# One row-block load of two weight matrices in a fused convolution and max-out kernel, and the order of its opening

## The chip, the core and the metric

The kernel runs on one core of a Trainium2 chip. The core has a matrix engine (TensorE, "PE" in the profile), a vector engine (VectorE, "DVE"), a scalar engine (ScalarE, "ACT"), GpSimd ("POOL") and SyncE ("SP"), which here only issues transfers. Sixteen DMA engines move data between memory (HBM) and the on-chip buffer SBUF; TensorE writes its results to PSUM, from which ScalarE and VectorE copy them. Each engine works through its own queue of instructions in order and waits on semaphores of the others. The metric is device time in microseconds for one launch, lower is better.

## What is computed

```python
def _attn_ref(x, weight_gen):            # x (8, 4160, 192), weight_gen (8, 4160, 8, 7)
    w = weight_gen - np.max(weight_gen, axis=-1, keepdims=True)
    w = np.exp(w)
    w = w / (np.sum(w, axis=-1, keepdims=True) + 1e-09)
    x_pad = np.concatenate([np.zeros((B, 6, D)), x], axis=1)
    idx = np.arange(S)[:, None] + np.arange(7)[None, :]
    x_unf = x_pad[:, idx, :].reshape(B, S, 7, 8, 24)
    return np.einsum('bshk,bskhg->bshg', w, x_unf).reshape(B, S, D)

def _moe_ref(x, w1, w2, w_out):          # w1, w2 (192, 1024), w_out (1024, 192)
    h1 = x @ w1
    h2 = x @ w2
    g = np.maximum(h1, h2)
    return g @ w_out
```

The second function is applied to the first one's result: a convolution over the last seven positions with weights that a softmax gives for each position and head, and then two products whose larger value, element by element, goes through a third. All arrays are float32; 33280 positions of 192 features in all.

## The kernel before

**Tiling.** The 33280 positions are laid on 128 partitions with 260 columns each. Columns are taken in 17 batches, of 16 columns but for the last two (12 and 8); batches 0 and 1 are cut into pieces of four columns, the later ones of eight. A batch goes through: an exponential of its weights (ScalarE, `exp_sum`, L153), a sum (VectorE, `red`, L168), a logarithm (ScalarE, `ln`, L172), a subtraction (VectorE, `shift`, L177) and a second exponential (ScalarE, `weights`, L191), which gives the softmax; then a product with seven shifted views of x (VectorE, `mul`, L211). For batches 0 and 1 the sum over the seven taps and the transposition are done by matmuls with an identity (`sum_transpose`, L281), copied out of PSUM by ScalarE (`sums_out`, L293).

**The max-out.** max(h1, h2) is computed as h1 + relu(h2 - h1). So w2 - w1 is formed on VectorE (`diff`, L593), the hidden product uses that difference (`hid_tile`, L336), ScalarE applies the relu (`relu`, L346), and the result is multiplied by w_out (`out_hidden`, L375). The h1 part needs only x @ (w1 @ w_out): w1 is cast (L611), transposed on TensorE (`w1_products`, L628), copied (L633), multiplied by w_out (`w10_product`, L647) and copied again (L654, L656), and enters at L387.

**The weights in blocks.** w1 and w2 have 192 rows of 1024 columns. Their first 128 rows go to one buffer each (`ws0E`, `ws1E`), in two halves of 512 columns (`load_w`, L562). The last 64 rows go to a second buffer of 128 partitions by 512 (`ws0T`, `ws1T`): columns 0 to 511 on partitions 0 to 63, columns 512 to 1023 on partitions 64 to 127, each by a transfer of its own (`load_last`, L570). `diff(i)` makes block i of the difference: 0 and 1 from the two halves of the first rows, 2 from the last rows. `wd` has six blocks of 512 columns; blocks 3, 4 and 5 are blocks 0, 1 and 2 with their partition halves exchanged, made by a matmul with a rotated identity into PSUM (`turn`, L601) and a copy out of it (`turn_out`, L607). Hidden features 0 to 511 read blocks 0, 2, 3 and 5; features 512 to 1023 read 1, 2, 4 and 5. With pieces of four columns a piece has four hidden tiles, of two feature chunks each: tiles 0 and 1 of a piece cover features 0 to 511, tiles 2 and 3 the others.

**What sets the order.** The kernel's engines follow the order in which the program names the steps. From batch 2's second half on this is a loop over groups of hidden tiles; up to there it is written out by hand in the string OPENING, whose steps are carried out one after the other, each adding instructions to its engines' queues. A step is a short name with numbers behind points; `@step` behind it makes it wait for another step. The names that matter here:

| Step | Engine | What |
|---|---|---|
| lg.b, xf, lw.h.i, lt.h.i | SP's queue (lg from batch 2 on: GpSimd's) | loads: weight_gen of batch b; x of the first piece (`xs`); first rows of w1 or w2 (i = 0, 1), half h; last rows, half h |
| lx.b.c.n, lh, lo | GpSimd's queue | loads: x of batch b, n columns from c; earlier columns; w_out |
| X, l, W | ScalarE | first exponential, logarithm, second exponential |
| n, s, m | VectorE | sum, subtraction, product |
| xa, xv | ScalarE, VectorE | cast of x's first piece |
| y.u, e.u | TensorE, ScalarE | sum over taps and transposition of piece u; its copy |
| d.i, t.i, T.i | VectorE, TensorE, ScalarE | difference, turned block, its copy (T.0: blocks 3 and 5 in one instruction; T.1: block 4) |
| c.i, v, V, p, C | ScalarE for c, V, C; TensorE for v, p | cast of w1, its transposition, copy, product with w_out, copy |
| h.t, r.t | TensorE, ScalarE | hidden tile t; its relu |
| A, B, D, E | TensorE, ScalarE, TensorE, ScalarE | output products, first part; a hand-over; second part; copy of the result |
| k.n | TensorE | n matmuls of the identity, whose result nobody reads (L663) |

PSUM has two buffers for h (and k) and two for y, t, v, p and A in the opening, so h.2 waits for r.0, and v for the buffer of a turned block.

Of the kernel before, what the change touches and what calls it, by code (L numbers as in the profile page):

```python
# [17 lines left out]
def _sub(base: bass.AP, off: int, dims):  # L18
    ap = [list(base.ap[0])] + [[int(s), int(c)] for s, c in dims]
    return dataclasses.replace(base, offset=base.offset + off, ap=ap)  # L20
# [3 lines left out]
def kernel(  # L24
# [9 lines left out]
    nc = tc.nc  # L34

    B, S, D = x.shape
    H, K = weight_gen.shape[2], weight_gen.shape[3]
    F = moe_w1.shape[1]
    P = 128
    PAD = K - 1  # L40
    WGC = H * K
    FCH = F // P
    HF = F // 2
# [220 lines left out]
    def half(j):  # L264
        return slice(64 * j, 64 * j + 64)
# [62 lines left out]
    def hid_tile(t):  # L328


        u = TILES[t][0]
        fs, w = chunks(t)
        for f in fs:
            for s in range(3):
                for j in range(2):
                    nc.tensor.matmul(  # L336
                        hid_out(t, f, j), lhsT=wd_at(j, s, f // 4, f % 4 * P, P),
                        rhs=_sub(yt_ts[u][half(j), :], (s + j) % 3 * P, [[3 * P, w // P], [1, P]]),
                        start=(f == fs[0] and s == 0), stop=(f == fs[-1] and s == 2),
                        skip_group_check=True,  # L340
                    )

    def relu(rd, t0, n):

        (hd, at), k = hd_at[t0], rd_at[t0][1]
        relu_of[t0] = nc.scalar.activation(out=rd[:, k * 1024:(k + n) * 1024], in_=hd[:, at:at + n * 1024],  # L346
                                           func=AF.Relu)

    def column(c):

        for u, (b, o, n) in enumerate(UNITS):
            k = c - BATCHES[b][0] - o
            if 0 <= k < n:
                return u, k // 2, k % 2
# [7 lines left out]
    def op_out(c):  # L362

        tile_, at = op_at[c // 2]
        return tile_[:, at + c % 2 * 512:at + c % 2 * 512 + D]

    def out_hidden(c, f, r):

        u, i, j = column(c)
        t0 = TILES.index((u, 0))  # L370
        if UNITS[u][2] == 8:
            (rd, k), at = rd_at[t0 + f], j * 512 + i * P
        else:
            (rd, k), at = rd_at[t0 + f // 2], j * 512 + f % 2 * 256 + i * P
        return nc.tensor.matmul(  # L375
            op_out(c), lhsT=rd[half(r), k * 1024 + at:k * 1024 + at + P],
            rhs=wo[half(r), f * D:(f + 1) * D], start=False, stop=(r != j and f == FCH - 1),
            skip_group_check=True,
        )

    def out_first(now):

        for c in now[::2]:
            u, i, _ = column(c)
            for s in range(3):
                for j in range(2):
                    nc.tensor.matmul(  # L387
                        op_out(c + j),
                        lhsT=yt_ts[u][half(j), (3 * i + (s + j) % 3) * P:(3 * i + (s + j) % 3 + 1) * P],
                        rhs=w10[half(j), s * D:(s + 1) * D], start=(c == now[0] and s == 0),  # L390
                        stop=False, skip_group_check=True,
                    )
            for f in range(FCH):
                last = [out_hidden(c + j, f, j) for j in range(2)]
        return last
# [10 lines left out]
    def relay(last):  # L406

        go = nc.scalar.nop()
        for mm in last:
            tc.add_manual_dep(go.ins, mm.ins.name, SYNC, reason="bank of the other half")  # L410
        return go
# [53 lines left out]
    OUTS, c = [[], [], []], 0  # L465
    for g in range(3, len(GROUPS)):
        most = 4 if g == 3 else 2 if GROUPS[g][1] == 2 or len(OUTS[-1]) == 4 else 4
        n = min(most, ready[g] - c)
# [5 lines left out]
    def room(g):  # L474

        t0, n = GROUPS[g]
        for t, k in zip(range(t0, t0 + n), "abc"[:n - 1] + "c"):
            hd_at[t] = ps[k].tile([P, 1024], FP32, name="hd" + k, tag=k), 0
        rd = prd.tile([P, 3 * 1024], BF16, name="rd_t", tag="rd")
        for t in range(t0, t0 + n):  # L480
            rd_at[t] = (rd, t - t0)
        return rd

    def out_room(now, tag=None):
        tag = tag or ("r" if "r" in ps else "o")
        tile_ = ps[tag].tile([P, 1024], FP32, name="op_ps", tag=tag if tag in "abc" else "op")
        for c in now:
            op_at[c // 2] = tile_, (c - now[0]) // 2 * D

    def hidden(g, now=(), between=lambda: None, beside=lambda: None, ahead=lambda: None,  # L490
               before=lambda: None, after=lambda: None):


        t0, n = GROUPS[g]
        rd = room(g)
        for t in range(t0, t0 + n - 1):
            hid_tile(t)
        if now:
            out_room(now, "a" if n == 1 and "a" in ps else None)
            last = out_first(now)  # L500
        for t in range(t0, t0 + n - 1):
            relu(rd, t, 1)
        if now:
            go = relay(last)
        hid_tile(t0 + n - 1)
        before()
        if len(now) > 2:
            beside()
        relu(rd, t0 + n - 1, 1)
        ahead()  # L510
        if now:
            out_second(now, go)
            evac(now[0] // 2, len(now) // 2)
        between()
        after()
        if len(now) <= 2:
            beside()
# [17 lines left out]
    wd = consts.tile([P, 3 * F], BF16, name="wd")  # L535
    wo = consts.tile([P, FCH * D], BF16, name="wo")
    w10 = consts.tile([P, 3 * D], BF16, name="w10")
# [10 lines left out]
    ws = {(kind, wi): stage.tile([P, w], FP32, name=f"ws{wi}{kind}") for kind, w in (("E", F), ("T", HF)) for wi in range(2)}  # L548
    w1 = stage.tile([P, F + HF], BF16, name="w1")
    w1t = stage.tile([P, FCH * D], BF16, name="w1t")  # L550
# [16 lines left out]
    def load_last(h, wi):  # L567

        wsrc = (moe_w1, moe_w2)[wi]
        return nc.sync.dma_start(  # L570
            out=ws["T", wi][half(h), :],
            in_=bass.AP(tensor=wsrc.tensor, offset=P * F + h * HF, ap=[[F, 64], [1, HF]]),
        )
# [8 lines left out]
    def block(i):  # L582

        return wd[:, i * HF:(i + 1) * HF]

    def features(i, wi):

        return (ws["T", wi] if i == 2 else ws["E", wi])[:, i % 2 * HF:(i % 2 + 1) * HF]
# [4 lines left out]
        return nc.vector.tensor_tensor(out=block(i), in0=a, in1=b, op=ALU.subtract)  # L593

    turned = {}

    def turn(i):

# [4 lines left out]

    def turn_out(i, v=0):

        n = 2 - i
        return (nc.vector.tensor_copy if v else nc.scalar.copy)(out=_sub(wd, (3 + i) * HF, [[2 * HF, n], [1, HF]]), in_=_sub(turned[i], 0, [[512, n], [1, HF]]))  # L607

    def cast_w1(i):

        return nc.scalar.copy(out=w1[:, i * HF:(i + 1) * HF], in_=features(i, 0))  # L611

    def w1_transposed(_):

# [13 lines left out]
                nc.tensor.matmul(tp[:, at:at + (64 if r else P)], lhsT=w1[rows, c0:c0 + P], rhs=ident[rows, rows],  # L628
                                 is_transpose=True, skip_group_check=True)

    def w1_copy(h):

        return nc.scalar.copy(out=w1t[:, 4 * h * D:4 * (h + 1) * D], in_=turned["v"][:, h * 1024:h * 1024 + 4 * D])  # L633

    def few(n):

# [10 lines left out]
                nc.tensor.matmul(pw[:, r * 512:r * 512 + D], lhsT=w1t[:, c0:c0 + P], rhs=wo[:, fi * D:(fi + 1) * D],  # L647
                                 start=(fi == 0), stop=(fi == FCH - 1), skip_group_check=True)

    def w10_copy(i):  # L650

        pw = turned["w"]
        if i == 0:
            return nc.scalar.copy(out=_sub(w10, 0, [[D, 2], [1, D]]), in_=_sub(pw, 0, [[512, 2], [1, D]]))  # L654
        to, frm, at = ((64, 0, 0), (0, 64, 512))[i - 1]
        return nc.scalar.copy(out=w10[to:to + 64, 2 * D:3 * D], in_=pw[frm:frm + 64, at:at + D])  # L656

    warm = ps["h"].tile([P, 1024], FP32, name="warm", tag="hd")

# [31 lines left out]
    def results_buffer(_):  # L691
# [16 lines left out]
    }  # L708

    OPENING = """  # L710
        lg.0 xf.-6.6 xf.0.4 lt.1.1 lt.0.0 lw.0.1 lw.0.0 lt.1.0 k.1 lw.1.1 lt.0.1 lw.1.0 lg.1 X.0.0.2 X.0.1.2
        n.0.0.2 n.0.1.2 l.0.0.2 l.0.1.2 s.0.0.2 k.1 W.0.0.0 s.0.1.2 xa.-6.4 W.0.0.1 W.0.8 xv.-2.6 k.19
        lx.0.4.4@l.0.0.2 lx.0.12.4@xa.-6.4 m.0.0.0 c.0 W.0.12 m.0.0.1 W.0.4 y.0.0 k.3 y.0.1 e.0.0 c.2 d.0 d.2
        e.0.1 t.0 k.2 c.1 t.2 k.4 T.0 d.1 t.1 k.2 T.1 m.0.4 lx.0.8.4@W.0.4 lo.0@e.0.0 lg.3@e.0.1 h.0 X.1 r.0
        h.1 r.1 lx.1.0.8@m.0.4 v.0 n.1 V.0 l.1 h.2 y.1 r.2 e.1 m.0.8 s.1 lg.2@r.2 m.0.12 h.3 r.3 h.4 h.5 V.1
        r.4 W.1.0 W.1.4 m.1.0 y.2 r.5 e.2 h.6 lx.1.8.8@W.1.0 m.1.4 p.0 C.2 h.7 y.3 C.1 lh.2 C.0 r.6 W.1.8 r.7
        X.2 n.2 A.3 m.1.8 e.3 B.3 h.8 D.3 r.8 Z.0 E.3 A.4 B.4 lx.2.0.8.0@r.8 h.9 l.2 X.3 W.1.12 y.4 e.4 r.9
        s.2 D.4 h.10 E.4 W.2.0 n.3 r.10 lg.4@r.10 A.5 y.5 h.11 e.5 l.3 m.1.12 B.5 r.11 D.5 h.12 E.5 A.6 B.6
        h.13 D.6 r.12 y.6 E.6 W.2.8 lx.2.8.8@W.2.8 r.13 A.7 e.6 h.14 h.15 B.7 r.14 r.15 D.7 y.7 E.7 e.7
    """  # L720

    make_identity(nc, ident_f)
# [91 lines left out]
```

## Time and profile before

| | |
|---|---|
| median of 3 runs | 411.23 us (407.48, 411.23, 412.59) |
| profiled execution, its own time | 407.24 us |
| its span, first to last instruction | 405.4 us |
| granted TensorE clock | 0.999 |
| TensorE's matmuls | 210.6 us at L375, 201.9 at L336 (the loop's three groups), 55.4 at L387 |
| VectorE's products, L211 | 187.5 us, 39 instructions |
| ScalarE's relus, L346 | 251.1 us (the loop's three groups) |
| moved by the DMA engines | 63.16 MB, mean 156 GB/s |

The page names groups by line, engine and what goes into and out of them. A window row gives its limits, its length, and the busy time (instructions) of PE, PEld (weight loads), DVE, ACT and POOL, then the granted clock, the mean busy share of the DMA engines and GB/s. Times to landing run from a transfer's issue to the last of its data. A matmul's end is modelled, so neighbouring rows can overlap a little.

### The profile page before, as it was taken

The numbers are of one execution on the slowest core, as the hardware profiler recorded it, in microseconds if no ns is written. First come the engines' busy times: TensorE is split into PE (matmuls) and PEld (weight loads), VectorE is DVE, ScalarE is ACT, GpSimd is POOL, SyncE is SP. The second block draws the span as 40 slices with busy tenths as digits, with TensorE's granted clock in tenths as the row PEclk, the third lists the DMA queues.
The fourth block names the chain that finished last, engine by engine and source line by source line (L and its number), as shares of the span: only waits on it lengthen the run. The fifth ranks groups of instructions, "written<-read, shape, count | busy, mean of one in ns | idle before, by whom it ended". The sixth has DMA issues, their size and how long they took to land.

```text
span 405.4 us, 16319 instructions
## 1 busy us (share of the span) xinstructions
PE 396.0 (98%) x7503; PEld 321.1 (79%) x7503; DVE 369.3 (91%) x211; ACT 361.1 (89%) x465; POOL 69.7 (17%) x96
## 2 busy tenths in 40 slices
PE   6999999999999999999999999999999999999996
PEld 2688999777777877777777778777777877787995
DVE  6999999999999999999999999999999999998200
ACT  5999899999999989999899999989999899888872
POOL 2211020212112211122220122121112121210100
PEclk9999999999999999999999999999999999999999
DMA  8955569765877656874776667778457847557304
GB/s 262 247 120 106 155 113 173 188 163 136 164 131 207 175 97 113 251 191 80 213 190 106 146 189 189 91 232 189 78 133 217 170 79 210 136 99 197 100 40 157
DMA packets 60019, 63.16 MB, mean 156 GB/s; under 512 B 47545, under 2 KB 48569, under 8 KB 59952
## 3 DMA queue, kind: packets, MB, share of 16 engines
q1 hardware_dynamic: 51952, 40.15, 37.7%
q0 software_dynamic: 7856, 21.89, 27.4%
q8 instruction: 58, 0.95, 0.9%
q10 hardware_dynamic: 144, 0.10, 0.1%
q14 instruction: 9, 0.07, 0.0%
HBM read 36.55 MB, written 25.56 MB: 153 GB/s over the span
## 4 chain that ended last, share of the span: by engine, by line
PE 94%; DMA 3%; ACT 2%; issue 0%; SPq 0%
PE op_ps L375 42%; PE hdc L336 13%; PE hdb L336 13%; PE hda L336 13%; PE op_ps L387 8%; PE yps L281 2%; PE hdp L336 2%; DMA ws0E<-in_moe_w_dram 1%; DMA xs<-in_x_dram 1%; ACT rd_t L346 1%; PE pw L647 0%; ACT wd L607 0%; ACT e_t L153 0%; ACT w1t L633 0%; ACT yt L293 0%
## 5 line engine op out<-in xcount | busy, mean ns | idle before, releaser
L375 PE MATMUL op_ps<-wo,rd_t 64*128 64x192 bf16 x4160 | 210.6, 243 | 0.6 <-issue 0.6
L375 PEld LDWEIGHTS <-rd_t 64*128 64x128 bf16 x4160 | 180.7, 94 | 15.6 <-issue 0.8
L211 DVE TENSOR_TENSOR m_t<-xb,en_t 128x10752 bf16<-128x10752 bf16 (+2 forms) x39 | 187.5, 4817 | 2.0 <-ACT en_t L191 1.9
L336 PEld LDWEIGHTS <-wd 64*128 64x128 bf16 x1824 | 96.3, 94 | 39.2 <-issue 1.9
L346 ACT ACTIVATE rd_t<-hdc 128x1024 bf16<-128x1024 f32 x82 | 84.0, 1025 | 18.1 <-PE hdc L336 16.5
L253 POOL CAST gate<-yt 128x1 f32<-128x1 bf16 x30 | 37.3, 1243 | 272.3 <-DMA yt<-y_t 272.3
L346 ACT ACTIVATE rd_t<-hdb 128x1024 bf16<-128x1024 f32 x81 | 83.7, 1033 | 0.0
L346 ACT ACTIVATE rd_t<-hda 128x1024 bf16<-128x1024 f32 x81 | 83.4, 1030 | 0.0
L227 DVE TENSOR_TENSOR m_t<-m_t 128x4608 bf16<-128x4608 bf16 (+1 forms) x30 | 72.9, 2431 | 0.1
L336 PE MATMUL hdc<-yt,wd 64*128 64x512 bf16 (+1 forms) x552 | 67.9, 353 | 0.0
L431 ACT COPY o_t<-op_ps 128x384 f32<-128x384 f32 (+1 forms) x99 | 56.0, 577 | 12.6 <-PE op_ps L375 12.6
L336 PE MATMUL hda<-yt,wd 64*128 64x512 bf16 (+1 forms) x540 | 67.0, 355 | 0.0
L336 PE MATMUL hdb<-yt,wd 64*128 64x512 bf16 (+1 forms) x540 | 67.0, 355 | 0.0
L387 PE MATMUL op_ps<-w,yt 64*128 64x192 bf16 x780 | 55.4, 243 | 0.0
L387 PEld LDWEIGHTS <-yt 64*128 64x128 bf16 x780 | 38.8, 94 | 14.6 <-issue 0.3
L233 DVE TENSOR_TENSOR m_t<-m_t 128x3072 bf16<-128x3072 bf16 (+1 forms) x30 | 50.1, 1671 | 0.1
L191 ACT ACTIVATE en_t<-wg_t 128x896 bf16<-128x896 f32 (+3 forms) x48 | 35.4, 769 | 2.3 <-PE op_ps L375 2.0
L236 DVE TENSOR_TENSOR y_t<-m_t 128x1536 bf16<-128x1536 bf16 (+1 forms) x30 | 27.4, 915 | 0.6
L168 DVE TENSOR_REDUCE sum_t<-e_t 128x64 f32<-128x448 f32 (+3 forms) x31 | 19.6, 635 | 3.2 <-ACT e_t L153 3.1
L125 POOL DMA_DIRECT2D xb<-in_x_dram x34 | 18.2, 535 | 24.0 <-ACT en_t L191 12.3
L177 DVE TENSOR_TENSOR wg_t<-wg_t,sum_t 128x280 f32<-128x280 f32 (+6 forms) x46 | 22.0, 480 | 0.0
L153 ACT ACTIVATE e_t<-wg_t 128x896 f32<-128x896 f32 (+2 forms) x18 | 15.8, 884 | 2.1 <-DMA wg_t<-in_weight_gen_dram 2.1
(39 smaller groups left out, 111.3 us busy)
## 6 DMA issues: line engine op xcount, KB each, us to landing
out_dram<-o_t SPq DMA_DIRECT2D x27, 768.0 KB, 4.8
xb<-in_x_dram POOLq DMA_DIRECT2D x30, 384.0 KB, 5.3
wg_t<-in_weight_gen_dram POOLq DMA_DIRECT2D x13, 448.0 KB, 6.0
out_dram<-o_t SPq DMA_DIRECT2D x10, 384.0 KB, 3.3
xb<-xb POOLq DMA_DIRECT2D x7, 288.0 KB, 5.1
wg_t<-in_weight_gen_dram SPq DMA_DIRECT2D x2, 448.0 KB, 5.5
xb<-in_x_dram POOLq DMA_DIRECT2D x4, 192.0 KB, 6.1
xs<-in_x_dram SPq DMA_DIRECT2D x1, 576.0 KB, 4.4
```

What stands on the lines that cost most here:

```text
L177: nc.vector.tensor_tensor(out=w_t, in0=w_t, in1=_sub(s_ts[b], hs.start, [[1, hs.stop - hs.start], [0, K]]), op=ALU.subtract)
L191: act = nc.scalar.activation(out=_sub(en_ts[b], (o * WGC + ((i or 0) * J + j) * N * K) * 2, [[2 * N, K], [2, N], [1, 2]]), in_=_sub(wg_ts[ ...
L211: return nc.vector.tensor_tensor(out=m_out, in0=x_in, in1=_sub(en_ts[b], at * H * 2, [[2, K * n * H], [0, G // 2], [1, 2]]), op=ALU.mult,)
L227: nc.vector.tensor_tensor(out=taps(0, 1, 3), in0=taps(0, 1, 3), in1=taps(3, 1, 3), op=ALU.add)
L233: nc.vector.tensor_tensor(out=taps(0, 2, 2), in0=taps(0, 2, 2), in1=taps(1, 5, 2), op=ALU.add)
L236: nc.vector.tensor_tensor(out=_sub(y_ts[b], o * D, [[64, 2], [P, 3 * w // 2], [1, 64]]), in0=taps(0, 1, 1), in1=taps(2, 1, 1), op=ALU.add,)
L253: nc.gpsimd.tensor_copy(out=gate, in_=yt[:, 0:1])
L336: nc.tensor.matmul(hid_out(t, f, j), lhsT=wd_at(j, s, f // 4, f % 4 * P, P), rhs=_sub(yt_ts[u][half(j), :], (s + j) % 3 * P, [[3 * P, w // ...
L346: relu_of[t0] = nc.scalar.activation(out=rd[:, k * 1024:(k + n) * 1024], in_=hd[:, at:at + n * 1024], func=AF.Relu)
L375: return nc.tensor.matmul(op_out(c), lhsT=rd[half(r), k * 1024 + at:k * 1024 + at + P], rhs=wo[half(r), f * D:(f + 1) * D], start=False, s ...
L387: nc.tensor.matmul(op_out(c + j), lhsT=yt_ts[u][half(j), (3 * i + (s + j) % 3) * P:(3 * i + (s + j) % 3 + 1) * P], rhs=w10[half(j), s * D: ...
L431: copied = nc.scalar.copy(out=_sub(o, c % 24 * D, [[D, len(qs)], [h * D, 2], [1, D]]), in_=_sub(tile_, at + (qs[0] - p) * D, [[D, len(qs)] ...
```

## The change

Three things are edited. `load_last` gets a form for h = 2 that loads both column halves of the last rows with one transfer onto 128 partitions, so OPENING has lt.2.1 and lt.2.0 in place of four steps. `turn_out` gets a form for i > 2 that copies one block alone, on ScalarE or, with a second argument, on VectorE: T.0 becomes T.3.1 (block 3, VectorE) and T.4 (block 5, ScalarE). And OPENING is written in another order, with other numbers of k and other waits behind the loads. Options that OPENING does not use (another engine for the casts and copies, a whole-partition form of `out_hidden`) are left out of the diff below, and so is a line of `hidden` that comes to the same.

```diff
@@ -567,6 +567,11 @@
     def load_last(h, wi):
 
         wsrc = (moe_w1, moe_w2)[wi]
+        if h == 2:
+            return nc.sync.dma_start(
+                out=ws["T", wi][:, :],
+                in_=bass.AP(tensor=wsrc.tensor, offset=P * F, ap=[[HF, 2], [F, 64], [1, HF]]),
+            )
         return nc.sync.dma_start(
             out=ws["T", wi][half(h), :],
             in_=bass.AP(tensor=wsrc.tensor, offset=P * F + h * HF, ap=[[F, 64], [1, HF]]),
...
@@ -603,12 +609,18 @@
 
     def turn_out(i, v=0):
 
+        to = (nc.vector.tensor_copy if v else nc.scalar.copy)
+        if i > 2:
+            k = i - 3
+            return to(out=block(3 + 2 * k), in_=turned[0][:, 512 * k:512 * k + HF])
         n = 2 - i
-        return (nc.vector.tensor_copy if v else nc.scalar.copy)(out=_sub(wd, (3 + i) * HF, [[2 * HF, n], [1, HF]]), in_=_sub(turned[i], 0, [[512, n], [1, HF]]))
-
-    def cast_w1(i):
-
-        return nc.scalar.copy(out=w1[:, i * HF:(i + 1) * HF], in_=features(i, 0))
+        return to(out=_sub(wd, (3 + i) * HF, [[2 * HF, n], [1, HF]]), in_=_sub(turned[i], 0, [[512, n], [1, HF]]))
+
+    def cast_w1(i, eng=0):
+
+        if eng == 3:
+            return nc.gpsimd.dma_start(out=w1[:, i * HF:(i + 1) * HF], in_=features(i, 0))
+        return ENG[eng](out=w1[:, i * HF:(i + 1) * HF], in_=features(i, 0))
 
     def w1_transposed(_):
...
@@ -708,15 +720,15 @@
     }
 
     OPENING = """
-        lg.0 xf.-6.6 xf.0.4 lt.1.1 lt.0.0 lw.0.1 lw.0.0 lt.1.0 k.1 lw.1.1 lt.0.1 lw.1.0 lg.1 X.0.0.2 X.0.1.2
-        n.0.0.2 n.0.1.2 l.0.0.2 l.0.1.2 s.0.0.2 k.1 W.0.0.0 s.0.1.2 xa.-6.4 W.0.0.1 W.0.8 xv.-2.6 k.19
-        lx.0.4.4@l.0.0.2 lx.0.12.4@xa.-6.4 m.0.0.0 c.0 W.0.12 m.0.0.1 W.0.4 y.0.0 k.3 y.0.1 e.0.0 c.2 d.0 d.2
-        e.0.1 t.0 k.2 c.1 t.2 k.4 T.0 d.1 t.1 k.2 T.1 m.0.4 lx.0.8.4@W.0.4 lo.0@e.0.0 lg.3@e.0.1 h.0 X.1 r.0
-        h.1 r.1 lx.1.0.8@m.0.4 v.0 n.1 V.0 l.1 h.2 y.1 r.2 e.1 m.0.8 s.1 lg.2@r.2 m.0.12 h.3 r.3 h.4 h.5 V.1
-        r.4 W.1.0 W.1.4 m.1.0 y.2 r.5 e.2 h.6 lx.1.8.8@W.1.0 m.1.4 p.0 C.2 h.7 y.3 C.1 lh.2 C.0 r.6 W.1.8 r.7
-        X.2 n.2 A.3 m.1.8 e.3 B.3 h.8 D.3 r.8 Z.0 E.3 A.4 B.4 lx.2.0.8.0@r.8 h.9 l.2 X.3 W.1.12 y.4 e.4 r.9
-        s.2 D.4 h.10 E.4 W.2.0 n.3 r.10 lg.4@r.10 A.5 y.5 h.11 e.5 l.3 m.1.12 B.5 r.11 D.5 h.12 E.5 A.6 B.6
-        h.13 D.6 r.12 y.6 E.6 W.2.8 lx.2.8.8@W.2.8 r.13 A.7 e.6 h.14 h.15 B.7 r.14 r.15 D.7 y.7 E.7 e.7
+        lg.0 xf.-6.6 xf.0.4 lt.2.1 lt.2.0 lw.0.1 lw.0.0 lw.1.0 lw.1.1 lg.1 X.0.0.2 k.2 X.0.1.2 n.0.0.2
+        n.0.1.2 l.0.0.2 k.1 l.0.1.2 s.0.0.2 W.0.0.0 k.19 s.0.1.2 xa.-6.4 xv.-2.6 lx.0.8.4@X.0.1.2 W.0.4
+        lx.0.4.4@xa.-6.4 m.0.0.0 W.0.0.1 W.0.12 y.0.0 m.0.0.1 W.0.8 k.3 d.0 y.0.1 lx.0.12.4 e.0.0 d.2 t.0
+        t.2 lg.2 k.1 c.0 T.3.1 e.0.1 k.2 T.4 h.0 d.1 h.1 c.2 c.1 t.1 r.0 T.1 m.0.4 X.1 m.0.8 r.1 lo.0 n.1
+        h.2 y.1 lg.3@X.1 h.3 r.2 e.1 v.0 lx.1.0.8@m.0.4 r.3 l.1 s.1 V.0 m.0.12 V.1 W.1.0 h.4 r.4 y.2 h.5
+        lx.1.8.8@l.1 p.0 m.1.0 r.5 h.6 e.2 C.2 h.7 C.0 C.1 X.2 lh.2 y.3 W.1.4 n.2 A.3 W.1.8 r.6 B.3 e.3 D.3
+        h.8 Z.0 r.7 m.1.4 E.3 W.1.12 l.2 r.8 X.3 A.4 y.4 e.4 B.4 lx.2.0.8.0@r.7 h.9 r.9 m.1.8 h.10 s.2 D.4
+        m.1.12 E.4 A.5 r.10 h.11 y.5 W.2.0 lg.4@r.9 e.5 n.3 B.5 r.11 h.12 D.5 E.5 r.12 A.6 B.6 h.13 l.3 D.6
+        lx.2.8.8@l.3 r.13 E.6 y.6 h.14 W.2.8 A.7 h.15 r.14 B.7 e.6 r.15 D.7 y.7 E.7 e.7
     """
 
     make_identity(nc, ident_f)
```

More of the change, by code (lines that the diff above doesn't have):

```diff
@@ L365, in op_out, with out_hidden @@
         return tile_[:, at + c % 2 * 512:at + c % 2 * 512 + D]
-    def out_hidden(c, f, r):
+    def out_hidden(c, f, r=None):
         u, i, j = column(c)
@@ L374, in out_hidden @@
             (rd, k), at = rd_at[t0 + f // 2], j * 512 + f % 2 * 256 + i * P
+        rows = slice(0, P) if r is None else half(r)
         return nc.tensor.matmul(
-            op_out(c), lhsT=rd[half(r), k * 1024 + at:k * 1024 + at + P],
-            rhs=wo[half(r), f * D:(f + 1) * D], start=False, stop=(r != j and f == FCH - 1),
+            op_out(c), lhsT=rd[rows, k * 1024 + at:k * 1024 + at + P],
+            rhs=wo[rows, f * D:(f + 1) * D], start=False, stop=(r != j and f == FCH - 1),
             skip_group_check=True,
@@ L502, in hidden @@
             relu(rd, t, 1)
-        if now:
-            go = relay(last)
+        go = relay(last) if now else None
         hid_tile(t0 + n - 1)
@@ L595 @@
     turned = {}
+    ENG = (nc.scalar.copy, nc.vector.tensor_copy, nc.gpsimd.tensor_copy)
     def turn(i):
@@ L629, in w1_products, with w1_copy @@
                                  is_transpose=True, skip_group_check=True)
-    def w1_copy(h):
-        return nc.scalar.copy(out=w1t[:, 4 * h * D:4 * (h + 1) * D], in_=turned["v"][:, h * 1024:h * 1024 + 4 * D])
+    def w1_copy(h, eng=0):
+        return ENG[eng](out=w1t[:, 4 * h * D:4 * (h + 1) * D], in_=turned["v"][:, h * 1024:h * 1024 + 4 * D])
     def few(n):
@@ L648, in w10_product, with w10_copy @@
                                  start=(fi == 0), stop=(fi == FCH - 1), skip_group_check=True)
-    def w10_copy(i):
+    def w10_copy(i, eng=0):
         pw = turned["w"]
         if i == 0:
-            return nc.scalar.copy(out=_sub(w10, 0, [[D, 2], [1, D]]), in_=_sub(pw, 0, [[512, 2], [1, D]]))
+            return ENG[eng](out=_sub(w10, 0, [[D, 2], [1, D]]), in_=_sub(pw, 0, [[512, 2], [1, D]]))
         to, frm, at = ((64, 0, 0), (0, 64, 512))[i - 1]
-        return nc.scalar.copy(out=w10[to:to + 64, 2 * D:3 * D], in_=pw[frm:frm + 64, at:at + D])
+        return ENG[eng](out=w10[to:to + 64, 2 * D:3 * D], in_=pw[frm:frm + 64, at:at + D])
     warm = ps["h"].tile([P, 1024], FP32, name="warm", tag="hd")
```

## The prediction

> **What bounds the kernel now.** I read the page's busy times and slices first, then the chain that ended last over the opening, then each engine's order there, and last the transfers.
>
> ```profile
> PE 396.0 (98%) x7503; PEld 321.1 (79%) x7503; DVE 369.3 (91%) x211; ACT 361.1 (89%) x465; POOL 69.7 (17%) x96
> ...
> PE   6999999999999999999999999999999999999996
> ```
>
> TensorE is busy in every slice but the first and the last, so work cannot be hidden anywhere else: a change to the opening is worth what it moves the point from which TensorE never stops. The chain over the first 22 us shows what leads to that point:
>
> ```profile
> 1.66 5.49 DMA xs<-in_x_dram
> 7.15 0.02 issue
> 7.16 6.03 DMA ws0E<-in_moe_w_dram
> 13.20 0.02 issue
> 13.22 0.62 ACT w L611
> 13.84 1.40 ACT wd L607 x2
> 15.24 0.94 ACT e_t L153
> 16.18 1.82 ACT rd_t L346 x2
> ```
>
> Columns are start, length, what. The loads set the first 13.2 us; ScalarE's queue the next 8 (it goes on so to 21.4); from 21.5 on the chain is TensorE. TensorE's own order shows the same turn (start, length, work):
>
> ```profile
> 12.14 0.59 PE L663 MATMUL warm<-around 128*128 128x512 bf16 x2
> 12.70 0.38 PE L601 MATMUL turned<-wd,around 128*128 128x512 bf16 x1
> 12.91 1.02 PE L663 MATMUL warm<-around 128*128 128x512 bf16 x4
> 14.04 0.39 PE L601 MATMUL turned<-wd,around 128*128 128x512 bf16 x1
> 14.27 0.59 PE L663 MATMUL warm<-around 128*128 128x512 bf16 x2
> 14.79 1.48 PE L336 MATMUL hdp<-yt,wd 64*128 64x256 bf16 x24
> ```
>
> L663 is filler; the first useful hidden tiles (h.0, h.1) start at 14.79. The transfers ahead of them:
>
> ```profile
> GB/s 0 0 0 108 158 308 438 422 415 381 396 352 291 238 246 266 377 344 205 274 310 204 229 342 387 323 317 257 230 241 142 161 169 167 302 359 292 157 157 229
> ...
> ws0E<-in_moe_w_dram SPq DMA_DIRECT2D x2, 256.0 KB, 6.0
> ...
> ws1T<-in_moe_w_dram SPq DMA_DIRECT2D x2, 128.0 KB, 5.9
> ```
>
> ```profile
> 4.00:8.00 4.00, 4.00 (x16) 1.68 (x15) 2.98 (x5) 3.10 (x10) 0.72 (x2) 1.00 1.03 323
> 8.00:12.00 4.00, 2.98 (x92) 1.74 (x90) 3.67 (x4) 2.72 (x9) 0.52 (x1) 1.00 1.08 286
> ```
>
> The GB/s row has half-microsecond slices of the first 20 us; the rows below it end in size and median us to landing; in the two window rows the last figures are the clock, the share of the 16 DMA engines (full) and GB/s. The engines are full from 4 us on, so bytes, not issues, set the landings. Issue plus time to landing gives them: xs 7.15, the four 64-row pieces 7.64, 8.22, 10.46, 11.93, the four 128-row halves of the first rows 8.76, 9.92, 11.69, 13.20.
>
> **The parts that cost little.** Two issues on SP's queue fall away (0.47 to 0.59 us each), and with them SP's wait of 1.1 us for xs ahead of the last weight load; that load is then issued near 5.0 instead of 7.16. Worth nothing by itself: the queue has work until 13.2 either way. If it ran dry, it would be worth up to 2 us.
>
> Do 64-row pieces load worse than 128-row ones? From one landing to the next the four pieces took 0.49, 0.58, 0.54 and 0.24 us, 1.85 for 0.52 MB; the four halves 0.54, 1.16, 1.23 and 1.27, 4.20 for 1.05 MB. Per byte the pieces lose nothing, so I put joining at 0. [...]
>
> T.0 (L607, both halves on ScalarE) becomes T.4 there and T.3.1 on VectorE. T.0 and T.1 took 1.40 us for three blocks, 0.47 each, so ScalarE saves about 0.5. VectorE has no copy out of PSUM in this trace: below, its cast of 1152 elements in 0.76 gives 0.34 for 512; above, its difference of 512 in 0.69. I take 0.65, as nearest in size. Behind it stand d.1 and m.0.4, which wait for loads anyway.
>
> Order: h.0 and h.1 no longer stand behind d.1, t.1 and T.1, whose blocks they don't read, and T.4 goes ahead of c.2 and c.1. So the first tiles need only the first halves and the last rows. Fillers behind y.0.1 go from 8 (2.2 us) to 3. On VectorE m.0.8 goes ahead of n.1, so l.1, V.0 and V.1 behind it on ScalarE may wait some 0.3 us, ahead of p.0.
>
> On GpSimd's queue the load for m.0.8 now goes first (released at 5.2 by the second exponential), that for m.0.4 second, that for m.0.12 third, and lg.2 and lo.0 follow with no wait, at about 9 to 10 instead of 20.1 and 12.59. Before, the first x load was issued at 5.96 and landed at 12.73, the second 7.98 to 15.33. m.0.4, at 13.90 now, would wait for the second: to 15.3, 1.4 us, if nothing else changes; to nothing, if the 0.8 us of earlier release and the freed SP queue pull it in.
>
> **The part that I think decides.** The joined load's source walks two column blocks (outermost dimension 2), then 64 rows, then 512 elements. All other loads of the opening have 64 or 128 rows outermost. No row of the trace has this form, so its price is bounded. Below, it runs on 16 engines like any 256 KB half and costs nothing. Above, each block is carried whole by one engine, and both loads use the same two. One engine moved 27.4 GB/s at the trace's best slice (438 over 16) and 20.2 in the window from 4 to 8 us (323 over 16). A block is 128 KiB, 131 KB: 4.8 to 6.5 us; two loads in a row 9.6 to 13.0.
>
> I take the upper end. The nearest rows by size are the 256 KB halves, but they aren't of this form: 128 or 64 shares can be dealt over 16 engines, two can't, and dealing by the outermost dimension is the simplest way that fits all the rows. [...]
>
> On those two engines everything later on SP's queue stands behind the blocks. xs is through at 7.15; the blocks add 9.6 (the better rate, since 14 engines leave the memory free); GpSimd's five loads, 0.39, 0.39, 0.39, 0.46 and 0.79 MB read, put 151 KB on each engine, 0 to 7.5 us there, of which I take 4.5 since both queues were served together from 10.2 to 13.2. So the second joined load lands at 21.3. Each 256 KB half then adds 16 KB, 0.6 us: ws0E's first half lands at 22.5, the last half at 23.7.
>
> VectorE does d.0, d.2 and T.3.1 from 22.5 (3 x 0.65), d.1 to 25.05, then m.0.4 in 2.9 (L211): y.1, TensorE's next work behind h.2, starts at 27.95 instead of 17.79: 10.2 later. All TensorE work behind it is kept, v.0's 0.85 joins it, and about as much of its idle time up to 21.5 goes. TensorE stands idle from about 12 to 24. It starts slowly: fillers came 0.43 us apart until 5.47 (weight-load rows at 4.62, 5.04, 5.47), then 0.21, though the granted clock reads 1.00. A second such start costs 0 to 1.5 us (half of 3.0); I take 1.0, since VectorE's chain covers part.
>
> Sum: 407.24 (405.4 of span, 1.8 around it) + 10.2 + 1.0 = 418.4. The runs' median, 411.23, is 4.0 above the profiled execution; a forecast of a median adds half of that: **420 us**. Bounds: no sharing with GpSimd's loads and no slow start, 16.8 for the blocks, 18.0 for the half, m.0.4 at 20.6, y.1 at 23.5: 5.7 later, 413. The lower rate and all of the sharing: 7.15 + 13.0 + 7.5 = 27.7, halves of 0.8, m.0.4 at 31.9, y.1 at 34.8: 17 later; with the slow start and the 4.0, 430. That needs all three together; I end the range at 427.
>
> **Rivals.** *All 16 engines carry the joined loads* (the change does what it says). Then bytes as before: last rows land by 8.8, the first halves by 11.0, the second by 13.2. d.0 starts at 11.05, t.2 at 12.4, h.0 near 13.4 instead of 14.79: 1.4 earlier. If the x load comes in time, about 0.9 of it survives to the end (h.2 must now wait for T.1): 406.3. For it: the SP rows show 256 KB loads landing in 6 us, whatever the order. Against it: the source's form. It decides if the joined loads land before 11.05, where VectorE comes free for d.0. Not slower: 406 to 408, or 410 to 412 beside the median.
>
> *16 engines, and the x load for m.0.4 comes late*, at 15.3: y.1 at 18.3 instead of 17.79, l.1 waits for n.1 behind m.0.8 (21.2 to 22.2) and holds V.0 and p.0: about 0.9 slower in the end, 408. It decides from 14.9 on, where m.0.4's 2.87 pass 17.79. For it: 7.4 us to landing for the second x load before.
>
> *Two engines, but GpSimd's loads stay out of the way*: 413 to 415, inside 2%.
>
> **How the numbers follow.** Two engines 0.70, of which a tenth lies above 427 and a seventh within 2%; 16 engines in time 0.16, late 0.13; 0.01 for more. The likeliest case's own range is 413 to 427; 408 to 427 takes in most of the 16-engine cases beside the median and leaves out about 0.15. Two per cent, about what a measurement of this kernel can tell from no change, is 8.2 us. Slower: 0.70 x 0.86 = 0.60. Faster needs 8.2 us gained ahead of h.0's 14.79, while d.0 cannot start before 10: 0.01. Within: 0.39.
>
> **What would show it.** Right: the two joined loads take 12 us or more to land; the second difference wait on VectorE names a ws tile; TensorE idle from 12 past 20; h.0 at 24 to 26; fillers or hidden tiles at half speed after it. Wrong: joined loads landing within 7 us and h.0 before 14.5. T.3.1 near 0.65 and no wait of ScalarE for it would bear out the small parts; a DMA wait ahead of m.0.4 the late x load.

## The result, and the profile after

| | before | after |
|---|---|---|
| median | 410.73 us (407.48 to 412.59, 4 runs) | 422.63 us (422.16 to 423.26, 4 runs) |
| profiled execution | 407.24 | 422.39 |
| span | 405.4 | 420.6 |
| granted clock | 0.999 | 0.979 |

After divided by before is 1.03, 95% interval 1.0231 to 1.0368: slower, by 15.15 us in the profiled executions. The first rows of the profile's page say where to look: the engines' busy times, then TensorE's busy share in 40 equal slices of the span.

```profile
PE 397.9 (95%) x7499; PEld 320.8 (76%) x7499; DVE 369.8 (88%) x212; ACT 360.9 (86%) x465; POOL 66.9 (16%) x96
...
PE   7149999999999999999999999999999999999996
```

Busy times have hardly moved (PE 396.0 before, 397.9 now); the span has grown by idle time in the second and third slices, 10.5 to 31.5 us. What released TensorE there is in the chain that ended last, cut to the first 36 us (start, length, what):

```profile
2.12 0.70 SPq L571
2.82 0.05 issue
2.87 0.51 SPq L571
3.38 0.04 issue
3.42 6.46 SPq L562
9.88 0.05 issue
9.93 15.67 DMA ws0E<-in_moe_w_dram
...
25.70 0.70 DVE wd L598
26.40 0.04 issue
26.44 0.58 PE turned L607
27.02 0.02 issue
27.04 0.59 PE turned L607
27.63 1.28 PE warm L675 x3
28.91 2.30 PE hdp L336 x24
```

L571 issues the two joined loads. Two things follow them. The issue of the next load, the first half of w2's first rows, holds SP for 6.46 us; and the load issued behind that one, the first half of w1's first rows, needs 15.67 us to land, where such a load took 6 before. What moved the data meanwhile? Two stretches of the run, from 6 to 10 us, with the columns of a window row (limits, length, busy time of PE, PEld, DVE, ACT, POOL, clock, mean busy share of the 16 DMA engines, GB/s):

```profile
6.00:8.00 2.00, 2.00 (x9) 0.81 (x8) 1.90 (x4) 1.70 (x6) 0.29 (x1) 1.00 0.56 101
8.00:10.00 2.00, 2.00 (x45) 1.03 (x43) 2.00 (x2) 1.96 (x8) 1.92 (x4) 1.00 0.57 101
```

and the transfers of those four microseconds by queue (packets, MB, share of 16 engines' time):

```profile
q0 software_dynamic: 158, 0.22, 44.6%
q1 hardware_dynamic: 91, 0.18, 11.9%
```

q1 is SP's queue, which carries all weights. 11.9% of 16 engines is 1.9 engines: two of them work for SP, at 0.18 MB in 4 us, some 22 GB/s each, and the other 14 have nothing from SP. Before, the same four microseconds moved 1.12 MB on that queue:

```profile
q1 hardware_dynamic: 638, 1.12, 104.9%
```

The semaphores of the loads say it once more, if a step of a load's semaphore is read as one DMA engine that is done. Every other load of the opening shows 16 separate steps; the joined ones show these (us), behind one early step each at 3.22 and 3.81, about 1 us after the issue and 10 us or more before the data, which is left out:

```
load                       steps by DMA engines     the other 14 engines done   all landed
w2's last rows, joined     13.73 13.96              -                           13.96
w1's last rows, joined     23.64 23.69              -                           23.69
w2's first rows, half 1    16                       16.5                        24.68
w1's first rows, half 1    16                       19.2                        25.60
w1's first rows, half 2    16                       20.3                        26.24
w2's first rows, half 2    16                       21.1                        26.91
```

So each block of 131 KB is carried by one engine, and every later load waits for its last two sixteenths. That it is two and not four says that both joined loads use the same two engines. VectorE's order behind it (start, length, work, and in brackets the idle time ahead and what ended it):

```profile
25.70 0.69 DVE L598 TENSOR_TENSOR wd<-ws1E,ws0E 128x512 bf16<-128x512 f32 x1 [14.84 <-DMA ws0E<-in_moe_w_dram]
26.30 0.68 DVE L598 TENSOR_TENSOR wd<-ws1T,ws0T 128x512 bf16<-128x512 f32 x1
27.67 0.69 DVE L615 CAST wd<-turned 128x512 bf16<-128x512 f32 x1 [0.68 <-PE turned L607]
28.27 0.68 DVE L598 TENSOR_TENSOR wd<-ws1E,ws0E 128x512 bf16<-128x512 f32 x1
28.87 5.82 DVE L211 TENSOR_TENSOR m_t<-xb,en_t 128x5376 bf16<-128x5376 bf16 x2
```

These are d.0, d.2, T.3.1, d.1 and m.0.4 with m.0.8. TensorE's order in the same stretch:

```profile
26.44 1.19 PE L607 MATMUL turned<-wd,around 128*128 128x512 bf16 x2 [14.72 <-DVE wd L598]
27.42 1.49 PE L675 MATMUL warm<-around 128*128 128x512 bf16 x3
28.84 2.36 PE L336 MATMUL hdp<-yt,wd 64*128 64x256 bf16 x24
...
32.20 0.72 PE L336 MATMUL hdp<-yt,wd 64*128 64x256 bf16 x10 [0.46 <-ACT wd L617]
32.76 1.39 PE L281 MATMUL yps<-around,m_t 64*128 64x64 bf16 x84
```

Before, y.1 stood here:

```profile
17.79 1.40 PE L281 MATMUL yps<-around,m_t 64*128 64x64 bf16 x84
```

It starts at 32.76 instead of 17.79: 14.97 later, nearly the whole 15.15. And TensorE comes back slowly: h.0 and h.1 take 2.36 us for what took 1.48. The granted clock shows why (third column from the end):

```profile
12.00:14.00 2.00, 0.00 (x0) 0.00 (x0) 0.00 (x0) 0.00 (x0) 0.00 (x0) 0.90 0.81 223
14.00:28.00 14.00, 1.54 (x4) 0.51 (x4) 1.63 (x3) 1.00 (x2) 0.00 (x0) 0.50 0.63 159
28.00:32.00 4.00, 3.74 (x30) 1.74 (x28) 4.00 (x4) 3.08 (x5) 0.00 (x0) 0.66 0.00 0
32.00:36.00 4.00, 3.79 (x130) 3.29 (x132) 3.69 (x2) 4.00 (x6) 1.08 (x2) 1.00 0.36 106
```

TensorE's last matmul ends near 11.7. In windows of one microsecond the clock reads 0.81 from 13 to 14, 0.50 from 14 to 30, 0.66 from 30 to 31, and 1.00 after.

### The profile page after: what moved, and what is told of

Its sections match the earlier page's. It is cut to its first block, busy times and chain, and to the rows that moved or that the text cites. A ratio compares the mean times of both kernels' runs of the same rounds, so it can differ in the third digit from the quotient of the medians.

```text
span 420.6 us, 16311 instructions
## 1 busy us (share of the span) xinstructions
PE 397.9 (95%) x7499; PEld 320.8 (76%) x7499; DVE 369.8 (88%) x212; ACT 360.9 (86%) x465; POOL 66.9 (16%) x96
## 4 chain that ended last, share of the span: by engine, by line
PE 89%; DMA 4%; ACT 3%; SPq 2%; issue 1%; DVE 0%; ACTq 0%; DVEq 0%
PE op_ps L376 40%; PE hdc L336 13%; PE hdb L336 12%; PE hda L336 12%; PE op_ps L388 8%; DMA ws0E<-in_moe_w_dram 4%; PE hdp L336 2%; SPq L562 2%; PE yps L281 1%; ACT rd_t L346 1%; ACT e_t L153 0%; ACT en_t L191 0%; ACT yt L293 0%; PE turned L607 0%; ACT w1t L645 0%
## 5 line engine op out<-in xcount | busy, mean ns | idle before, releaser
L253 POOL CAST gate<-yt 128x1 f32<-128x1 bf16 x30 | 34.2, 1139 | 278.5 <-DMA yt<-y_t 278.5
L153 ACT ACTIVATE e_t<-wg_t 128x896 f32<-128x896 f32 (+2 forms) x18 | 15.9, 888 | 2.2 <-DMA wg_t<-in_weight_gen_dram 2.2
```

What stands on the lines that cost most here:

```text
L253: nc.gpsimd.tensor_copy(out=gate, in_=yt[:, 0:1])
```

## The experiments

The kernel before ran beside each of these on the same chip; ratios are to those runs.

**The last rows in four pieces again, all else as changed.** Is it the joined load, or the new order?

```diff
-        lg.0 xf.-6.6 xf.0.4 lt.2.1 lt.2.0 lw.0.1 lw.0.0 ...
+        lg.0 xf.-6.6 xf.0.4 lt.0.1 lt.1.1 lt.0.0 lt.1.0 lw.0.1 lw.0.0 ...
```

> The changed kernel with its two joined loads taken apart again into four 64-row loads at the same place in SP's queue; everything else of the change stays. Theory (two engines carry a joined load, and all behind it in SP's queue waits): the loss goes. Last weights land by 13.5 us, h.0 near 13.4, the time is 406 to 408 in the profiled execution; 406 if the x load for m.0.4 is there by 14, 408 if it lands at 15.3. Rival (the new order of the opening, the copy on VectorE or the earlier loads of GpSimd cost it): h.0 past 20 and 415 or more.

Measured: 408.64 us (408.09 to 410.27, 12 runs), ratio 1.0002, interval 0.9982 to 1.0022. The four pieces landed at 7.25, 7.74, 8.27 and 8.81, the last half at 12.19. TensorE's order, with h.0, the rest of h.0 and h.1, and y.1:

```profile
13.46 0.48 PE L336 MATMUL hdp<-yt,wd 64*128 64x256 bf16 x3
14.28 1.37 PE L336 MATMUL hdp<-yt,wd 64*128 64x256 bf16 x21 [0.34 <-ACT wd L615]
...
17.51 1.40 PE L281 MATMUL yps<-around,m_t 64*128 64x64 bf16 x84
```

Without the joined load the whole loss is gone. The rest of the change brings h.0 1.3 us forward, of which y.1 keeps 0.3 and the time nothing that can be measured.

**The joined loads alone, in the order of before.**

```diff
+        if h == 2:
+            return nc.sync.dma_start(
+                out=ws["T", wi][:, :],
+                in_=bass.AP(tensor=wsrc.tensor, offset=P * F, ap=[[HF, 2], [F, 64], [1, HF]]),
+            )
...
-        lg.0 xf.-6.6 xf.0.4 lt.1.1 lt.0.0 lw.0.1 lw.0.0 lt.1.0 k.1 lw.1.1 lt.0.1 lw.1.0 lg.1 ...
+        lg.0 xf.-6.6 xf.0.4 lt.2.1 lt.2.0 lw.0.1 lw.0.0 k.1 lw.1.1 lw.1.0 lg.1 ...
```

> The kernel before with the joined loads alone: the first two 64-row loads become the two joined ones, the other two go; order, copies and GpSimd's loads as before. Theory: the loss comes with them. Joined loads land after 13 and after 20 us, ws0E's first half at 22 to 26, and the time is 418 to 424. Fewer loads stand on GpSimd's queue early here (two instead of five), so it may be 2 to 4 us less than the 422.4 of the changed kernel. Rival (the rest of the change costs it): within 2 us of the kernel before.

Measured: 418.23 us (418.06 to 418.76, 4 runs), ratio 1.0245, interval 1.0199 to 1.0291. The joined loads landed at 13.75 and 19.74, the last half at 22.41; y.1 started at 28.93. The joined loads alone make most of the loss. The second lands 4 us sooner here than in the changed kernel, whose order sends all of GpSimd's loads out early; the first lands only 0.2 sooner.

**The same bytes with 128 in the source's outermost place.** The joined transfer keeps its size, its 128 partitions and its place in the queue; it walks the same 256 KB in rows of 2 KB one behind the other, so the rows come to lie in other partitions and the result is another one.

```diff
-                in_=bass.AP(tensor=wsrc.tensor, offset=P * F, ap=[[HF, 2], [F, 64], [1, HF]]),
+                in_=bass.AP(tensor=wsrc.tensor, offset=P * F, ap=[[HF, 128], [1, HF]]),
```

> The changed kernel with the joined loads reading the same bytes as 128 rows of 512 elements one after the other (outermost dimension 128) instead of two blocks of 64 rows. The rows then stand in other partitions, so the last rows' part of the products is another one; the instructions and sizes are the same. Theory: 16 engines carry it, landing within 7 us, 406 to 408, the same as with four pieces to within 1 us. Rival (a load of 128 partitions and 256 KB early in SP's queue is what holds it up, whatever its form): 418 or more.

Measured: 407.09 us (406.87 to 408.46, 10 runs), ratio 0.9971, interval 0.9949 to 0.9993. The window from 6 to 8 us, in the columns of above, and the queues from 6 to 10 us:

```profile
6.00:8.00 2.00, 2.00 (x9) 0.82 (x8) 1.90 (x4) 1.72 (x6) 0.23 (x1) 1.00 1.05 374
```

```profile
q1 hardware_dynamic: 807, 1.47, 100.7%
q0 software_dynamic: 19, 0.03, 4.0%
```

All 16 engines are full with SP's loads, 1.47 MB where the changed kernel moved 0.18. So neither the size nor the 128 partitions is at fault; the order in which the source is walked is. (This walk also has a dimension less; the next two keep three.) The joined loads landed at 7.30 and 7.95, the second 1.41 us after xs (6.54), where the four pieces took 2.05 from xs (6.76) to the last. Joining on 16 engines is worth 0.64 us of landing, and y.1 comes at 16.83 instead of 17.51; the 0.29 that m.0.4 waited there for its x is gone here too.

**Four blocks and eight blocks.** If the outermost dimension sets the engines, 4 and 8 there must give 4 and 8. The blocks overlap in the source, so these versions too compute another result with the same amount of work.

```diff
-                in_=bass.AP(tensor=wsrc.tensor, offset=P * F, ap=[[HF, 2], [F, 64], [1, HF]]),
+                in_=bass.AP(tensor=wsrc.tensor, offset=P * F, ap=[[P, 4], [F, 32], [1, HF]]),
```

```diff
-                in_=bass.AP(tensor=wsrc.tensor, offset=P * F, ap=[[HF, 2], [F, 64], [1, HF]]),
+                in_=bass.AP(tensor=wsrc.tensor, offset=P * F, ap=[[64, 8], [F, 16], [1, HF]]),
```

> The changed kernel with the joined loads reading four blocks of 32 rows (outermost dimension 4, blocks 128 columns apart and overlapping) instead of two of 64: the same bytes on the same partitions, other data, so the last rows' part of the products is another one. Theory (as many engines as blocks): each of four engines carries 2 x 66 KB instead of 2 x 131 KB, the joined loads land at half the delay, near 10 and 15 us, the last halves near 17, and 6 to 8 of the 15.2 us remain: 413 to 415. Rival (a fixed cost of a pattern of three dimensions, in SP's issue or anywhere): no change from 422.

> As with four blocks, but eight of 16 rows, 64 columns apart (outermost dimension 8): the same bytes on the same partitions, other data, so the last rows' part of the products is another one. Theory (as many engines as blocks): each of eight engines carries 2 x 33 KB; by what the four engines took for 66 KB (4.8 and 6.1 us) the joined loads land near 9 and 12 us, the last halves near 14, and 1 to 4 us of the loss remain: 410 to 413. Rival (the count of engines isn't it): 417 or more, as with four.

Measured: with four 417.34 us (416.94 to 418.02, 4 runs), ratio 1.0221, interval 1.0181 to 1.026; with eight 410.71 us (410.3 to 411.69, 4 runs), ratio 1.0065, interval 1.0047 to 1.0082. The semaphores showed four and eight steps by DMA engines. Ratios stand in brackets, since the versions did not all run beside the same runs of the kernel before.

```
outermost    engines    second joined load landed    last half landed    time
2            2          23.69                        26.91               422.63 (1.0300)
4            4          17.50                        22.28               417.34 (1.0221)
8            8          11.48                        17.19               410.71 (1.0065)
128          16          7.95                        11.29               407.09 (0.9971)
```

The count of engines is as expected, and the time follows it. The size was not: with four blocks I had expected landings near 10 and 15, and halves that then cost little. From the first joined load's landing to the second's, an engine of these kernels got 131 KB in 9.73 us (two), 65.5 KB in 6.13 (four) and 32.8 KB in 2.60 (eight): 13.5, 10.7 and 12.6 GB/s. GpSimd's loads had 79.1% of the engines' time in that stretch with four blocks, but 3.5% with eight: they are not all of the reason there. The packets themselves got slower: one of 2048 bytes on SP's queue took 84 ns on the mean in the changed kernel (6.6 to 8.5 us), 131 with four blocks (6.6 to 10) and 143 with eight (8.9 to 11.4), the last two with hardly a packet of GpSimd's beside them. Why is open.

**GpSimd's loads held back.** What is that sharing worth? First three of the five loads (x for m.0.12, w_out, the next weights) wait until d.2, that is until the joined loads are through; then all five.

```diff
-        ... lx.0.12.4 e.0.0 d.2 t.0 t.2 lg.2 k.1 c.0 ... m.0.8 r.1 lo.0 n.1
+        ... e.0.0 d.2 t.0 t.2 k.1 c.0 ... m.0.8 r.1 lx.0.12.4@d.2 lo.0 lg.2 n.1
```

```diff
-        ... xv.-2.6 lx.0.8.4@X.0.1.2 W.0.4 lx.0.4.4@xa.-6.4 m.0.0.0 ... y.0.1 lx.0.12.4 e.0.0 d.2 t.0 t.2 lg.2 k.1 c.0 T.3.1 e.0.1 k.2 T.4 ... m.0.8 r.1 lo.0 n.1
+        ... xv.-2.6 W.0.4 m.0.0.0 ... y.0.1 e.0.0 d.2 t.0 t.2 k.1 c.0 T.3.1 e.0.1 lx.0.4.4@d.2 lx.0.8.4 lx.0.12.4 lo.0 lg.2 k.2 T.4 ... m.0.8 r.1 n.1
```

> The changed kernel with three of GpSimd's five early loads (x for m.0.12, w_out, weight_gen of batch 2) held until d.2 is done. Theory (GpSimd's loads share the two engines with the joined loads, the term that I put at 4.5 us): the second joined load lands near 20 us instead of 23.7, as with the kernel before plus the joined loads, where two such loads were out; h.0 at 24 to 26 instead of 28.8, and the time is 417.5 to 420 in the profiled execution. Rival (the two engines are slow by themselves, sharing costs nothing): landing past 23 and 421.5 to 423.

> The changed kernel with all five of GpSimd's early loads held until d.2 is done, to measure the two engines with nothing beside the joined loads. The time is not the question, since m.0.4 then waits for x. If one engine moves 27.4 GB/s, as the sum had it, the joined loads land near 11.4 and 16.2 us; if it moves 17 GB/s, as the first block did in the changed kernel (131 KB from 6.3 to 13.9), near 14 and 21.5.

Measured, one execution each and so with no interval: 419.17 us with three held, second joined load at 20.26; 420.47 with all five, joined loads at 12.86 and 18.39. The second kernel's time is no measure of the loss, since its m.0.4 waits for x; its landings are. From 12.86 to 18.39 each of the two engines moves 131 KB with nothing of GpSimd's beside it: 23.7 GB/s, between the 17 and the 27.4 that I had named. So GpSimd's loads add 23.69 - 18.39 = 5.3 us to the second landing, and nearly halve the rate of the two engines while they are out. SP's issue was held for 5.29 us here too (7.14 with three): GpSimd isn't the cause of that.

**Fillers through the idle time.** 66 matmuls nobody reads, ahead of the first turned block, so that the clock doesn't fall.

```diff
-        ... lx.0.12.4 e.0.0 d.2 t.0
+        ... lx.0.12.4 e.0.0 d.2 k.66 t.0
```

> The changed kernel with 66 more fillers on TensorE ahead of t.0, 14 us of them, which end before its wait does. Theory (the idle stretch costs a slow start, the term that I put at 1.0 us): the granted clock stays at 1.00, h.0 and h.1 take 1.5 us together instead of 2.4, and 1 to 2 us of the loss go: ratio to the kernel before 1.025 to 1.028 instead of 1.030. Rival (VectorE's products set the pace there and cover it): within 0.3 us of the changed kernel.

Measured: 422.13 us (421.94 to 422.33, 4 runs), ratio 1.0343, interval 1.0326 to 1.036, granted clock 0.999. TensorE's order:

```profile
11.45 14.42 PE L675 MATMUL warm<-around 128*128 128x512 bf16 x66
26.36 0.38 PE L607 MATMUL turned<-wd,around 128*128 128x512 bf16 x1 [0.49 <-DVE wd L598]
...
27.92 0.49 PE L336 MATMUL hdp<-yt,wd 64*128 64x256 bf16 x3
...
31.74 1.39 PE L281 MATMUL yps<-around,m_t 64*128 64x64 bf16 x84
```

The turned blocks and hidden tiles are back at their full speed, and y.1 starts 1.02 us sooner than in the changed kernel (d.0, which waits for the weights, starts 0.08 sooner). The end doesn't: the spans are 420.2 and 420.6, one execution each, and the two kernels' ratio intervals overlap. I had expected 1 to 2 us; the rival, a gain of less, is nearer. At 48 us ScalarE is still 0.9 ahead (its exponential of L153 at 48.35 against 49.25); where that goes afterwards is open.

**The small parts, on the four-piece version.** First, x for m.0.4 ahead of x for m.0.8 on GpSimd's queue; second, both turned blocks copied by one ScalarE instruction; third, both edits.

```diff
-        ... xv.-2.6 lx.0.8.4@X.0.1.2 W.0.4 lx.0.4.4@xa.-6.4 m.0.0.0 ...
+        ... xv.-2.6 lx.0.4.4@X.0.1.2 W.0.4 lx.0.8.4@xa.-6.4 m.0.0.0 ...
```

```diff
-        t.2 lg.2 k.1 c.0 T.3.1 e.0.1 k.2 T.4 h.0 d.1 h.1 ...
+        t.2 lg.2 k.1 c.0 e.0.1 k.2 T.0 h.0 d.1 h.1 ...
```

> As the four-piece version, but the x load for m.0.4 goes first on GpSimd's queue (released by X.0.1.2), that for m.0.8 second (released by the cast of x's first piece). In the four-piece version m.0.4 waited 0.29 us for its x, which landed at 14.47, the other at 11.54. Theory: m.0.4 then starts at 14.21, y.1 is 0.3 us earlier, m.0.8's x (landing near 14.5) is in time, and the time is 408.3 against 408.6, ratio to the kernel before 0.998 to 1.000. Rival: y.1 is held by h.2 or l.1 rather than by m.0.4, and the time stays within 0.1 us of the four-piece version's.

> As the four-piece version, but block 3 and block 5 are copied by one ScalarE instruction (T.0, 0.9 to 1.0 us) instead of T.3.1 on VectorE (0.69) and T.4 on ScalarE (0.58). In the four-piece version T.4 started only when T.3.1 had ended (12.92 to 13.61, then 13.64 to 14.22): the two copies ran one after the other, 1.30 us from the first's start. Theory (they exclude each other, so splitting gains nothing on that path): T.0 runs 12.9 to 13.9, d.1 0.7 earlier on VectorE, h.1 no later, the time the same or up to 0.5 us shorter: 408.1 to 408.7. Rival (VectorE's copy is what lets h.0 start early, and ScalarE has other work): h.0 starts 0.3 to 0.4 later than 13.46 and the time is 0.3 to 0.5 us longer, 409.

> Both of the last two edits. Theory: their gains add, m.0.4 starts near 13.8 when its x comes (landing near 12 to 13.8) and the time is 407.6 to 408.2, ratio 0.996 to 0.999. Rival: y.1 is held by h.2, whose block T.1 copies, and the time is that of the better of the two alone.

| | time (12 runs each) | ratio | interval |
|---|---|---|---|
| x first | 407.82 (407.09 to 408.67) | 0.9971 | 0.995 to 0.9991 |
| one copy on ScalarE | 408.64 (408.36 to 409.17) | 0.9986 | 0.9965 to 1.0007 |
| both | 407.72 (406.74 to 409.46) | 0.9975 | 0.9953 to 0.9996 |

The kernel before had 408.90 (406.92 to 411.51, 29 runs) beside them. The four-piece version's copies, T.3.1 and T.4:

```profile
12.92 0.69 DVE L615 CAST wd<-turned 128x512 bf16<-128x512 f32 x1 [0.75 <-PE turned L607]
13.64 0.58 ACT L615 CAST wd<-turned 128x512 bf16<-128x512 f32 x1 [0.78 <-DVE wd L615]
```

and VectorE's m.0.4 with x first, then with one copy on ScalarE:

```profile
13.92 5.82 DVE L211 TENSOR_TENSOR m_t<-xb,en_t 128x5376 bf16<-128x5376 bf16 x2
```

```profile
14.73 5.83 DVE L211 TENSOR_TENSOR m_t<-xb,en_t 128x5376 bf16<-128x5376 bf16 x2 [1.37 <-DMA xb<-in_x_dram]
```

With x first the wait ahead of m.0.4 is gone, m.0.4 starts 0.58 sooner (0.29 of it the wait that I had named), and y.1 comes at 17.08. That version is faster than the kernel before by 0.1 to 0.5%, and its median lies below the 408.3 that I had expected. With one copy the pair ends after 1.01 us instead of 1.30, and VectorE is free sooner; but then x is what m.0.4 waits for, and the time stays. With both, 407.72 is in the range that the theory gave, and it is as well the time of the better edit alone, as the rival has it: twelve runs don't tell these apart.

## Why the prediction was right, and where its sizes were off

The step that I thought decides did: the source's outermost dimension of 2 puts each joined load on two engines, the same two for both, and SP's later loads stand behind them. The counts of steps, 2, 4, 8 and 16 for an outermost dimension of 2, 4, 8 and 128, show it. The forecast, 420, is 2.6 below the median of 422.63 and inside the range. Of the signs that I had named, the long landings, the idle TensorE and the half speed behind it came; h.0 came later than 24 to 26, at 28.84, and VectorE's long wait stands ahead of its first difference, not the second. Of the sum, from y.1 back:

| term | put at | measured | off by |
|---|---|---|---|
| blocks on the two engines, without GpSimd | second load at 16.75 | 18.39 (all five held) | +1.6 |
| sharing with GpSimd's loads | 4.5 | 5.3 | +0.8 |
| from there to the first half of w1's first rows | 1.2 | 1.91 | +0.7 |
| from there to m.0.4 | 2.55 | 3.27 | +0.7 |
| from m.0.4 to y.1 | 2.90 | 3.89 | +1.0 |

The five add up to 4.8: y.1 at 32.76 instead of 27.95. One microsecond of that stood in the sum already, as the slow restart, so the sum was short by 4.0.

- **The rate** is the largest miss. I took 27.4 GB/s for one engine, the best slice of 16 busy ones, on the reasoning that 14 idle engines leave memory free. One engine alone gave 23.7. The lower bound that I named, 20.2, was as near.
- **The sharing** lay between my bounds of 0 and 7.5. It was argued from bytes; the runs show it as a nearly halved rate.
- **The halves** took 0.92 to 0.99 each at first instead of 0.6, and 0.64 and 0.67 later.
- **VectorE's queue**: I let T.3.1 follow d.2 at once, but it waits 0.68 for the turned blocks, and 0.47 even at full clock (with the fillers). Its own 0.69 was put at 0.65.
- **The slow restart** I put at 1.0, as a term beside y.1. It is that by size, 1.02 at y.1, and its place is from m.0.4 on: h.0 and h.1 hold t.1, T.1 and h.2, so y.1 stands behind h.2 on TensorE and not behind m.0.4. I took its slowness from the spacing of the fillers; the granted clock now shows it, 0.50. The 1.00 that I quoted beside that spacing is no reading: the trace before has no clock record ahead of 5.56 us, and a window without one shows 1.00. Of the 1.02, the spans with and without fillers show 0.4 at the end, one execution each.
- **Half of the median's offset**, 2.0, was not there: the changed kernel's four runs lie within 1.1 us, their median 0.24 above the profiled one. By luck that hid nearly half of the miss in the sum (418.4 against 422.39).

**The parts that cost little.** The new order, the split copies and the fewer fillers are together worth nothing that can be measured: the four-piece version has them, and its ratio is 1.0002. SP's shorter queue it does not have; of those on 16 engines only the version walked in one run does, with the last weight load issued at 4.57 instead of 6.78. The DMA engines were full in both from 6 to 8 us (share 1.05 and 1.07), so the issues don't seem to set the landings there, but the shorter queue was not tried by itself. That joining is worth 0 by itself was wrong: on 16 engines it gains 0.64 us of landing. The four pieces take 1.45 times as long for their bytes as the same bytes on 128 partitions, and their packets are slower too: 124 ns for 2048 bytes on the mean from 6.8 to 8.8 us, where the 128-row halves behind them took 94 (8.9 to 12) and the joined loads in one run 92 (6.6 to 7.9). Why the pieces are slower is not shown. My row-by-row comparison in the trace of before, where pieces and halves are mixed and landings overlap, could not show the gain.

That ScalarE saves about 0.5 by the copy on VectorE was wrong in its use: T.4 waits on VectorE's semaphore and starts when T.3.1 has ended (12.92 + 0.69 = 13.61, T.4 at 13.64), so the two follow each other. This is a wait of the program; what it guards, and whether two separate tiles would remove it, wasn't tried. The late x load was seen: 0.29 us ahead of m.0.4 in the four-piece version, where I had allowed up to 1.4. l.1 waited 0.40 for n.1, where I had said 0.3.

**The rivals.** With 16 engines the two rivals gave +/- 0.9 us. The four-piece version, the nearest to them that computes the same, lies between: 0.3 us gained at y.1, nothing in the time. That GpSimd's loads stay out of the way, 413 to 415, fell: they cost 5.3 us.

**Not on my list:** SP's issue held for 6.46 us. What holds it is not shown, nor was it tried by itself. It leaves 14 engines without weights from 6 to 10 us. That it costs nothing more is argued: on the two engines that land last, the loads follow each other without a gap from 13.73 to 26.91.

## What to carry to other kernels

Before two transfers are made one, look at the outermost dimension of the source, too, and not only at the partitions of the destination, which were 128 in all these runs: with 2, 4 or 8 there, the transfer ran on that many DMA engines, and everything behind it in the same queue waited for those. In these traces this showed as a load whose semaphore has few steps, a DMA share below one in a stretch that should be full (0.56, 0.80 and 0.70 from 6 to 8 us with 2, 4 and 8, against 1.05 with 128), and, only with 2, an issue on SP of 5.3 to 7.2 us. And price a stage by the landing of its last load, not by the mean rate: the 14 idle engines had finished their shares up to 8 us earlier.

## What the runs showed that I had not expected

- An issue on SP took 5.3 to 7.2 us where it followed two loads that ran on two engines, 0.48 where they ran on four.
- With four blocks the engines are slow even where GpSimd moves nothing: from 6 to 10 us SP's queue has a share of 91.0% and moves 0.90 MB, against 1.47 MB at 100.7% with the source walked in one run. The packets take longer, 131 ns against 92 in the stretches above; why was not settled.
- One of two engines got 23.7 GB/s with GpSimd's loads held back and 13.5 with them out.
- The granted clock fell to 0.50 while TensorE stood idle from 11.7 to 26.4 us, and that cost about 1.0 us at y.1, but the spans with and without the fillers differ by 0.4 of 420 us.
